# A planner's costs for the products with V are set to other values, and the whole order is searched again

## The chip, the cores and the metric

The kernel runs on one core of a Trainium2 chip. The metric is the device time of one execution in microseconds (us). Besides it there is a profile of one execution, taken by the hardware profiler: its span runs from the first to the last instruction, and the execution's own time is a little longer than the span.

## The reference, cut to what matters

Two independent parts are computed from different inputs and set side by side in the output, in float32:

```python
# A: attention, S = 2048 rows, D = 1024, H = 32 heads of 32
qkv = (x @ wqkv)                      # split into q, k, v by head
p = softmax(einsum("bhqd,bhkd->bhqk", q, k) * 32 ** -0.5)
o = einsum("bhqk,bhkd->bhqd", p, v)
a = o.reshape(B, S, D) @ wo
# B: real part of a two-dimensional Fourier transform by four matrices
u = einsum("bsd,ed->bse", xb, dft_hid_re); w = einsum("bsd,ed->bse", xb, dft_hid_im)
b = einsum("ts,bse->bte", dft_seq_re, u) - einsum("ts,bse->bte", dft_seq_im, w)
out = concatenate([a, b], -1)
```

## The kernel before

All dense products (q, k and v, the Fourier products, the product with wo) are done by a fast scheme with fewer block products (seven for eight, nested), and each product of float32 tiles is three matmuls of a high and a low half (hi*hi, lo*hi, hi*lo) into one PSUM bank. In the profile these matmuls have line L457. They are called fills here; there are 6528, each with 512 moving columns, and they stand in one list `fills` in a fixed order. What a fill reads is made ahead of it: a load by a queue of SyncE (SP), sums by DVE or POOL (L522), the high half by a cast on ACT (L542) or DVE (L544), the low half by a subtraction on POOL or DVE (L547). The tiles are called slot (moving) and hl (stationary).

The attention runs at the same time, head by head, and is three streams of PE work:

- S (L1896): 32 pairs of matmuls a head, scores of 128 queries against 1024 keys into one of two psS tiles. DVE takes the row maximum (L1902), ACT the exponent with a sum (L1905, an ACTIVATE and a read of the accumulator), after which the tile is free for the S pair after next. S only finds maxima and sums. Most pairs read their queries from the tile qs, the first four rows of a head from qx.
- T (L2018): 64 matmuls a head, the transposed scores less the maximum, one at a time into one of two psT banks. ACT takes the exponent (L2022) into a tile pt.
- V (L2037): the products with v. They stand in runs, three to a head, of 5, 5 and 6 key tiles (`ENDS`); a key tile is four matmuls in four column groups of 32 of the array, and the profile shows each of these as two. A run of 5 tiles is thus x40 in the profile and x20 in the program.

Every instruction is an `Op` with a cost in us, an engine and what it waits for. A planner (`Plan`, `run`) goes through time by these costs and decides which instruction comes next on each engine: whenever PE is free it takes a fill, or the head of one of the streams S, T and V, by readiness and some rules. What it writes is a fixed order for each engine. On the chip the engines go through their orders one instruction after another, and semaphores hold an instruction until its inputs are there; the planned times themselves are not used on the chip.

A fill that is not ready by the plan is passed over, and PE goes on with S and T alone. A place where T follows T with no fill between them, next to an S and not just behind a run of V, is called a bare pair here.

The planner's rules have eight numbers that a random search tunes: 90 trials (`TRIALS`), each a dry run of the whole plan, and the one with the shortest planned total is emitted. Two of the eight: `LATE` is the margin that PE leaves after an operand's planned readiness, and `RES` is how many fills are kept for the end. The cost of a run of V enters in two ways:

```python
v = op("PE", SWITCH + (t + 1 - t0) * PV, pv, [*load[: t // 4 + 1], *(x[3] for x in todo)], [vuse, *(x[4] for x in todo)])
ATT = H * (128 * MS + 16 * PV + 3 * SWITCH)
if fill is not None and (not ok or (not first and left <= HB) or nf / (FILL - RES) <= done / ATT):
```

The second of them is the total planned PE time of the attention, by which the fills are spread over it.

Of the kernel before, what the change touches and what calls it, by code (L numbers as in the profile page):

```python
# [253 lines left out]
def kernel(  # L254
# [128 lines left out]
    ORDER = (1, 2, 5, 6, 7, 3, 4)  # L383
    OUTERS = [(0, q) for q in (1, 5, 6, 7, 3, 2, 4)] + [(1, q) for q in ORDER]
    TWO = {(1, q) for q in ORDER} | {(0, 2), (0, 4)}
    MM, MS, PV, SWITCH, TINY = 0.2165, 0.2165, 0.853, 0.40, 0.17
    ES, ET = 1.222, 0.61
    MAX, EVAC, CAST, BIT = 1.22, 0.685, 0.415, 0.275
    SUB = 1.31
# [1843 lines left out]
```

## Time and profile before

| | |
|---|---|
| median of 3 runs | 2829.85 us (2828.16 to 2834.0) |
| the profiled execution, its own time | 2831.55 us |
| its span | 2829.8 us |
| PE busy | 2797.1 us (99%) |
| DVE busy, ACT busy, POOL busy | 2377.2, 2355.6, 1191.7 us |
| bytes moved by DMA | 768.18 MB, mean 271 GB/s |
| mean granted TensorE clock | 0.998 |

A busy share is the time in which at least one instruction of the engine is under way. Matmuls overlap in the profile, one of 512 columns being shown for 380 ns or so while the next one starts some 216 ns after it. How much of PE's time is lost is therefore read from the starts of the matmuls.

### The profile page before, as it was taken

How to read it: one execution, taken by the hardware profiler on the slowest of the kernel's cores; microseconds unless marked ns; L12 is line 12 of the kernel's file. 1: busy time of each engine (PE TensorE's matmuls, PEld its weight loads, DVE VectorE, ACT ScalarE, POOL GpSimd, SP SyncE). 2: the span in 40 equal slices, each digit the busy share in tenths (PEclk: the TensorE clock that was granted, in tenths of full speed). 3: DMA queues.
4: the chain of work that ended last, by engine and by line, in shares of the span. 5: the costliest groups of instructions: out<-in, count | busy, mean ns of one | idle time of the engine just before them, and what ended most of it. 6: DMA issues, size and time to landing. Idle time of an engine off the chain costs nothing.

```text
span 2829.8 us, 47069 instructions
## 1 busy us (share of the span) xinstructions
PE 2797.1 (99%) x14728; PEld 2095.6 (74%) x14728; DVE 2377.2 (84%) x3300; ACT 2355.6 (83%) x4490; POOL 1191.7 (42%) x945
## 2 busy tenths in 40 slices
PE   9999999999999999999999999999999999999999
PEld 8787777776777777677676777767767777777777
DVE  6678888788888888798988899888888998888845
ACT  5348898998899899889999988999988988888851
POOL 2234434133234432356545446676765331343300
PEclk9999999999999999999999999999999999999999
DMA  9989978798899988977999767888867665677548
GB/s 345 344 312 305 316 249 293 252 337 298 300 302 344 333 298 297 296 232 231 335 342 339 251 207 241 293 270 266 277 179 237 220 211 185 203 237 252 178 154 296
DMA packets 485844, 768.18 MB, mean 271 GB/s; under 512 B 120382, under 2 KB 153406, under 8 KB 485470
## 3 DMA queue, kind: packets, MB, share of 16 engines
q1 hardware_dynamic: 485452, 765.04, 81.6%
q8 instruction: 119, 1.95, 0.3%
q14 instruction: 129, 1.06, 0.1%
q10 hardware_dynamic: 144, 0.13, 0.0%
HBM read 511.74 MB, written 253.25 MB: 270 GB/s over the span
## 4 chain that ended last, share of the span: by engine, by line
PE 88%; DMA 5%; ACT 3%; DVE 2%; issue 1%; POOL 1%; SPq 1%; DVEq 0%; POOLq 0%; ACTq 0%
PE pd L457 40%; PE pd L2037 15%; PE psT L2018 15%; PE psS L1896 14%; PE psT L457 4%; ACT psS L1905 2%; ACT pt L2022 1%; DVE negm L1902 1%; DMA ha_d<-slot 1%; DMA ha_d<-c 0%; DMA c<-in_xb 0%; DMA raw<-in_xa 0%; DMA slot<-in_ct 0%; DMA qs<-qk_d 0%; DMA raw<-in_wv 0%
## 5 line engine op out<-in xcount | busy, mean ns | idle before, releaser
L457 PE MATMUL pd<-slot,hl 128*128 128x512 f32 x5088 | 1412.1, 380 | 4.0 <-ACT hl L542 2.0
L2022 ACT ACTIVATE pt<-psT 128x512 f32<-128x512 f32 x2048 | 1215.3, 689 | 228.8 <-PE psT L2018 227.3
L1902 DVE TENSOR_REDUCE negm<-psS 128x1 f32<-128x1024 f32 x1024 | 1241.5, 1219 | 169.2 <-PE psS L1896 153.8
L1905 ACT ACTIVATE psS<-psS,negm 128x1024 f32<-128x1024 f32 x1024 | 1225.1, 1197 | 41.6 <-DVE negm L1902 40.7
L457 PEld LDWEIGHTS pd<-slot,hl 128*128 128x128 f32 x5088 | 963.8, 190 | 133.3 <-ACT hl L542 2.4
L2018 PE MATMUL psT<-qs,ks 128*128 128x512 f32 x2048 | 786.0, 387 | 1.2 <-DMA r_d<-ll 0.7
L2018 PEld LDWEIGHTS psT<-qs,ks 128*128 128x128 f32 x2048 | 383.2, 188 | 168.8 <-issue 46.9
L1896 PE MATMUL psS<-ks,qs 128*128 128x512 f32 x1552 | 457.9, 381 | 9.1 <-ACT psS L1905 8.9
L2037 PE MATMUL pd<-pt,vt 128*32 128x512 f32 x4096 | 459.3, 594 | 2.8 <-DVE e L766 1.8
L547 POOL TENSOR_TENSOR slot<-raw,slot 128x512 fp32r<-128x512 f32 x153 | 194.9, 1279 | 353.8 <-DVE slot L547 98.8
L547 POOL TENSOR_TENSOR slot<-slot,slot 128x512 fp32r<-128x512 f32 x206 | 260.4, 1280 | 196.3 <-DVE slot L544 50.1
L1896 PEld LDWEIGHTS psS<-ks,qs 128*128 128x128 f32 x1552 | 283.7, 189 | 66.4 <-ACT psS L1905 21.3
L2037 PEld LDWEIGHTS pd<-pt,vt 128*32 128x32 f32 x4096 | 123.9, 110 | 281.4 <-issue 261.3
L1905 ACT ACTIVATION_READ_ACCUMULATOR psS<-psS,negm 128x1 f32 x1024 | 324.8, 317 | 0.0
L522 POOL TENSOR_TENSOR raw<-raw,g 128x512 f32<-128x512 f32 x114 | 145.4, 1279 | 231.9 <-DMA g<-tg_d 23.6
L547 POOL TENSOR_TENSOR hl<-raw,hl 128x512 fp32r<-128x512 f32 x113 | 144.4, 1279 | 214.8 <-PE psT L2018 62.0
L457 PE MATMUL pd<-slot,slot 128*128 128x512 f32 x780 | 200.8, 379 | 0.0
L457 PEld LDWEIGHTS pd<-slot,slot 128*128 128x128 f32 x780 | 147.4, 189 | 20.1
L1896 PE MATMUL psS<-ks,qx 128*128 128x512 f32 x496 | 146.5, 386 | 6.1 <-ACT psS L1905 5.3
L1896 PEld LDWEIGHTS psS<-ks,qx 128*128 128x128 f32 x496 | 90.0, 189 | 34.9 <-ACT psS L1905 10.9
L522 DVE TENSOR_TENSOR raw<-raw,g 128x512 f32<-128x512 f32 x146 | 106.9, 740 | 9.1 <-issue 2.2
L2050 DVE TENSOR_TENSOR ot<-ot,pd 128x512 f32<-128x512 f32 x64 | 43.9, 686 | 68.7 <-PE pd L2037 67.9
(139 smaller groups left out, 2135.0 us busy)
## 6 DMA issues: line engine op xcount, KB each, us to landing
hl<-ha_d SPq DMA_DIRECT2D x134, 512.0 KB
slot<-in_ct SPq DMA_DIRECT2D x144, 256.0 KB
qk_d<-e SPq DMA_DIRECT2D x52, 512.0 KB
qs<-qk_d SPq DMA_DIRECT2D x128, 192.0 KB
ks<-qk_d SPq DMA_DIRECT2D x128, 192.0 KB
raw<-g_d SPq DMA_DIRECT2D x96, 256.0 KB
ha_d<-hl SPq DMA_DIRECT2D x42, 512.0 KB
raw<-in_ct SPq DMA_DIRECT2D x80, 256.0 KB
```

Of the source, the lines that this page charges most:

```text
L457: nc.tensor.matmul(box["ps"], a[1]((a[0].hi, a[0].lo)[u]()), turns((b[0].hi, b[0].lo)[v]()), start=k == 0, stop=k == n - 1)
L522: (nc.gpsimd if e == "POOL" else nc.vector).tensor_tensor(out=dest(), in0=dest() if a is None else a.get(), in1=other["q"] if "q" in other ...
L547: (nc.gpsimd if e == "POOL" else nc.vector).tensor_tensor(out=lo(), in0=raw(), in1=f(hi()), op=ALU.subtract)
L1896: nc.tensor.matmul(p[:, i * NB : i * NB + NB], (QX[0] if own else QS[h % 2])[:, qt * P : qt * P + P], turns(KS[h % 2][:, c * 1024 + i * NB ...
L1902: nc.vector.tensor_reduce(out=ST["negm"][:, c, qt : qt + 1], in_=box["p"], axis=AX.X, op=ALU.max, negate=True)
L1905: nc.scalar.activation(box["p"], box["p"], AF.Exp, bias=ST["negm"][:, c, qt : qt + 1], accum_out=ST["sums"][:, c, qt : qt + 1])
L2018: nc.tensor.matmul(box["p"], KS[h % 2][:, t * P : t * P + P], turns(QS[h % 2][:, j * NB : j * NB + NB]), start=True, stop=True)
L2022: nc.scalar.activation(box["t"], box["p"], AF.Exp)
L2037: nc.tensor.matmul(po["p"][j * DH : j * DH + DH, :], VT[h][:, k, :], box["t"], start=(k == t0), stop=(k == t), tile_position=(0, j * DH),)
L2050: nc.vector.tensor_tensor(out=as_two(po["o"]), in0=as_two(po["o"]), in1=order_of(po["p"]), op=ALU.add)
```

## The change

Two costs of the planner get other values: `PV`, a key tile of a run of V, and `SWITCH`, what a run costs beyond its tiles. Nothing else in the source differs.

```diff
-    MM, MS, PV, SWITCH, TINY = 0.2165, 0.2165, 0.853, 0.40, 0.17
+    MM, MS, PV, SWITCH, TINY = 0.2165, 0.2165, 0.858, 0.337, 0.17
```

A run of 5 tiles is planned at 0.337 + 5 x 0.858 = 4.627 us, where it was 0.40 + 5 x 0.853 = 4.665; a run of 6 at 5.485, where it was 5.518. As every planned time behind the first run moves, the dry runs come out differently and the search ends at another trial: before it took `LATE` 0.239 and `SST` 13.89 (a ratio of the streams S and T) with the other six at their defaults (`RES` 700), now it takes `LATE` 0.177 and `RES` 567 with the others at their defaults. The instructions are the same except where an operation may go to one of two engines (ACT has 18 more, DVE 20 fewer, POOL 2 more); their order differs on every engine. On PE there are 21 bare pairs before and 29 now; 351 fills stand behind the last instruction of the attention before, 307 now.

On PE, near fill 2976 of 6528, where the group of fills that reads slot_14254 begins (slot_14293 is the same tile in the new program). Before:

```order
L457 MATMUL pd<-slot_13722,hl 128x512
L1896 MATMUL psS<-ks_2705,qs_2704 128x512 x2
L2018 MATMUL psT<-qs_709,ks_710 128x512
L457 MATMUL pd<-slot_13722,hl 128x512
L2018 MATMUL psT<-qs_709,ks_710 128x512
L457 MATMUL pd<-slot_13722,hl 128x512
L457 MATMUL pd<-slot_14254,hl 128x512 x2
L1896 MATMUL psS<-ks_2705,qs_2704 128x512 x2
L457 MATMUL pd<-slot_14254,hl 128x512
```

Now, at the same fills:

```order
L457 MATMUL pd<-slot_13702,hl 128x512
L2018 MATMUL psT<-qs_709,ks_710 128x512
L1896 MATMUL psS<-ks_2708,qx 128x512 x2
L2018 MATMUL psT<-qs_709,ks_710 128x512 x2
L1896 MATMUL psS<-ks_2708,qs_2707 128x512 x2
L2018 MATMUL psT<-qs_709,ks_710 128x512 x2
L1896 MATMUL psS<-ks_2708,qs_2707 128x512 x2
L2018 MATMUL psT<-qs_709,ks_710 128x512 x2
L1896 MATMUL psS<-ks_2708,qs_2707 128x512 x2
L2018 MATMUL psT<-qs_709,ks_710 128x512
L457 MATMUL pd<-slot_14293,hl 128x512 x2
```

Four S pairs and eight T stand where there were fills between them: three bare pairs.

On PE, at fill 3301, eleven fills ahead of a place at fill 3312 where four bare pairs stand in both orders (slot_15744 before and slot_15785 now are one tile). Before:

```order
L457 MATMUL pd<-slot_15744,hl 128x512
L1896 MATMUL psS<-ks_2705,qs_2704 128x512 x2
L2018 MATMUL psT<-qs_709,ks_710 128x512
L457 MATMUL pd<-slot_15744,hl 128x512
L2018 MATMUL psT<-qs_709,ks_710 128x512
L457 MATMUL pd<-slot_15744,hl 128x512
```

Now:

```order
L457 MATMUL pd<-slot_15785,hl 128x512
L1896 MATMUL psS<-ks_2708,qx 128x512 x2
L2018 MATMUL psT<-qs_709,ks_710 128x512 x2
L1896 MATMUL psS<-ks_2708,qx 128x512 x2
L2018 MATMUL psT<-qs_709,ks_710 128x512 x2
L1896 MATMUL psS<-ks_2708,qs_2707 128x512 x2
L2018 MATMUL psT<-qs_709,ks_710 128x512
L457 MATMUL pd<-slot_15785,hl 128x512 x2
```

The last two of these three fills now stand behind three S pairs and five T, with two bare pairs among them.

On ACT, where the scores of the second head begin; each L1905 is the exponent of one S pair, and the casts L542 make operands of fills. Before:

```order
L1905 ACTIVATE psS,sums<-psS,negm 128x1024 x3
L542 ACTIVATE slot_3026<-raw 128x512
L542 ACTIVATE hl<-raw 128x512
L1905 ACTIVATE psS,sums<-psS,negm 128x1024 x2
L1961 ACTIVATE tt<-tt 128x32
```

Now:

```order
L1905 ACTIVATE psS,sums<-psS,negm 128x1024 x2
L542 ACTIVATE slot_3028<-raw 128x512
L1905 ACTIVATE psS,sums<-psS,negm 128x1024
L542 ACTIVATE e<-e 128x512
L1334 ACTIVATE c<-c 128x512
L542 ACTIVATE hl<-raw 128x512
L1905 ACTIVATE psS,sums<-psS,negm 128x1024
```

The first cast to hl stood ahead of the 32nd exponent and now stands behind it, ahead of the 33rd.

## Rows read from the trace of the kernel before

**Rows 1.** The page: span, and PE (busy us, share, instructions).

```profile
span 2829.8 us, 47069 instructions
PE 2797.1 (99%) x14728; PEld 2095.6 (74%) x14728; DVE 2377.2 (84%) x3300; ACT 2355.6 (83%) x4490; POOL 1191.7 (42%) x945
```

**Rows 2.** Groups by line, PE: the products with V.

```profile
L2037 PE MATMUL pd<-pt,vt 128*32 128x512 f32 x4096 | 459.3, 594 | 2.8 <-DVE e L766 1.8 <-DVE slot L714 0.8 <-DVE e L1012 0.2
```

**Rows 3.** Timeline of PE after the attention: start us, us, what, count.

```profile
2755.55 10.52 PE L457 MATMUL pd<-slot,hl 128*128 128x512 f32 x48
2765.91 10.52 PE L457 MATMUL psT<-slot,hl 128*128 128x512 f32 x48
...
2821.59 1.46 PE L457 MATMUL pd<-slot,slot 128*128 128x512 f32 x6
```

**Rows 4.** Timeline of PE around one run of V of six tiles.

```profile
2368.00 0.81 PE L457 MATMUL pd<-slot,slot 128*128 128x512 f32 x3
2368.74 5.36 PE L2037 MATMUL pd<-pt,vt 128*32 128x512 f32 x48
2374.03 0.70 PE L2018 MATMUL psT<-qs,ks 128*128 128x512 f32 x2
2374.56 1.03 PE L1896 MATMUL psS<-ks,qx 128*128 128x512 f32 x4
```

**Rows 5.** Timeline of PE in the four bare pairs at fill 3312.

```profile
1366.24 0.92 PE L2018 MATMUL psT<-qs,ks 128*128 128x512 f32 x2
1367.77 0.70 PE L1896 MATMUL psS<-ks,qs 128*128 128x512 f32 x2 [0.61 <-ACT psS L1905]
1368.31 0.92 PE L2018 MATMUL psT<-qs,ks 128*128 128x512 f32 x2
1369.84 0.70 PE L1896 MATMUL psS<-ks,qs 128*128 128x512 f32 x2 [0.61 <-ACT psS L1905]
```

**Rows 6.** Timeline of ACT in the same stretch, one cycle.

```profile
1366.41 1.19 ACT L1905 ACTIVATE psS<-psS,negm 128x1024 f32<-128x1024 f32 x1
1367.41 0.31 ACT L1905 ACTIVATION_READ_ACCUMULATOR psS<-psS,negm 128x1 f32 x1
1367.50 1.19 ACT L2022 ACTIVATE pt<-psT 128x512 f32<-128x512 f32 x2
1368.46 1.21 ACT L1905 ACTIVATE psS<-psS,negm 128x1024 f32<-128x1024 f32 x1
```

**Rows 7.** Windows, PE alone: stretch, length, busy (matmuls), clock, DMA share, GB/s.

```profile
1129.30:1133.70 4.40, 3.17 (x10) 1.00 0.89 279
1364.20:1371.20 7.00, 5.33 (x17) 1.00 1.07 343
...
1888.50:1891.10 2.60, 1.97 (x6) 1.00 0.90 332
...
116.00:136.00 20.00, 15.45 (x59) 0.91 1.01 353
238.00:248.00 10.00, 7.43 (x27) 0.83 0.90 319
```

**Rows 8.** PE's waits over the whole span: total us, times, longest.

```profile
PE psS L1896 <- ACT psS L1905: 14.2, 23, 2.6
```

**Rows 9.** Timeline of PE, two waits within 116 to 136 us.

```profile
119.02 0.48 PE L457 MATMUL pd<-slot,hl 128*128 128x512 f32 x1 [1.99 <-ACT hl L542]
...
128.46 2.64 PE L457 MATMUL psT<-slot,hl 128*128 128x512 f32 x11 [1.27 <-DVE hl L547]
```

**Rows 10.** Timeline of all engines where the second head's scores begin.

```profile
237.93 2.84 SPq L506 DMA_DIRECT2D raw<-in_wqk  x2
...
240.91 0.63 ACT L542 ACTIVATE hl<-raw 128x512 fp32r<-128x512 f32 x1 [1.85 <-DMA raw<-in_wqk]
241.45 1.07 ACT L1905 ACTIVATE psS<-psS,negm 128x1024 f32<-128x1024 f32 x1
...
242.69 0.48 PE L1896 MATMUL psS<-ks,qx 128*128 128x512 f32 x1 [2.57 <-ACT psS L1905]
```

## Prediction

> **What bounds the kernel now.** I read the page first. TensorE (PE) is busy 99% of the span, 2797.1 of 2829.8 us, and ACT and DVE 83 and 84% [rows 1]. So PE sets the time, but its busy share says too little about what can still move: the profile shows a matmul for some 380 ns while the next one starts after 216. The timeline after the attention gives the pitch: 48 fills take 2765.91 - 2755.55 = 10.36 us, 0.2158 us each [rows 3]. Next I looked at one run of V. The three fills ahead of it should be done issuing at 2368.00 + 3 x 0.2158 = 2368.65; V starts at 2368.74, 0.09 later; it lasts until 2374.03, 5.29 us for six tiles; the two T behind it take 0.53 us where two pitches are 0.43, so leaving costs another 0.10 [rows 4]. Together 5.48 us.
>
> With these, all the work of PE can be added up. Of 14728 matmuls 4096 are V [rows 1, 2]. The other 10632 at 0.2158 us are 2294.4 us. V is 512 tiles at 0.858 and 96 runs at 0.337, 471.7 us. The sum is 2766.1 us; the span holds 63.7 us more. Of these 6.8 lie behind PE's last matmul, which ends at 2821.59 + 1.46 = 2823.05 [rows 3], and the rest is lost by PE. The change can only work on this rest, because it adds and removes no matmul.
>
> The Trainium skill (Perfetto Trace Analysis, Identifying the Most-Contended Engine) says that matmul busy time is a poor measure of what PE has left, since the instructions are pipelined. The rows here agree: by busy time 32.7 us are open, by the starts 63.7.
>
> Where is it lost? Three kinds of place stand out.
>
> (a) Bare pairs. Where no fill stands between S and T, PE runs into ACT. One cycle of ACT is one exponent, its accumulator read and two exponents of T: from 1366.41 to 1368.46, 2.05 us [rows 6]. PE starts an S pair every 2.07 us there and has only four matmuls, 0.86 us, to do in it [rows 5]. A full bare cycle thus loses 1.2 us. By windows: at fill 3312 four bare pairs take 7.00 us with 17 matmuls, 3.67 us of work, so 3.33 are lost, 0.83 a pair (the first one is cheap, since ACT is not behind yet). At 1129 us two pairs lose 4.40 - 10 x 0.2158 = 2.24, 1.12 each; at 1888 us one loses 2.60 - 6 x 0.2158 = 1.30 [rows 7].
>
> (b) The early stretch, where DMA is full (share 1.01): 116 to 136 us holds 59 matmuls, 12.7 us of work in 20, so 7.3 are lost; 238 to 248 us holds 27, so 4.2 are lost [rows 7]. In the first, PE waits for operands (1.99 and 1.27 us) [rows 9]. In the second, ACT's cast to hl waits for its weights, the exponent of an S pair stands behind it, and PE waits 2.57 us for that exponent [rows 10]. In both the granted clock falls, to means of 0.91 and 0.83 [rows 7]: that is 0.09 x 20 = 1.8 and 0.17 x 10 = 1.7 us, already within the losses.
>
> (c) Single waits elsewhere; the list has 23 waits of S for ACT, 14.2 us, the longest 2.6, bare pairs included [rows 8].
>
> **The change, part by part.** The table itself. The new values are right: a run of six tiles is planned at 5.485 us, measured 5.48, before 5.518 [rows 4]. The plan's clock no longer gains 0.033 to 0.038 us a run on the chip's, over 96 runs 3.5 us. On the chip this is worth nothing in itself, 0 us: a run lasts as long as it lasts, and semaphores set both clocks together again at each wait. What hides the old error is that a fixed order with waits needs no clock; 0.04 us is a fifth of one matmul. So the 3.5 us that leave the planned total do not leave the chip's.
>
> The new order: bare pairs. What reaches the chip is another order, found by a search that goes by the planned total. On PE it has 29 bare pairs in place of 21. The new ones are three at fill 2976, two at fill 3301 (ahead of the four at 3312, which stay), and more in ones and twos; some late ones are gone. Price of a pair: nothing, if the chip would have waited at that place anyway; 1.2 us at most, a full cycle [rows 5]; the three windows gave 0.83, 1.12 and 1.30 [rows 7]. I take 0.9, the lower part, because several of the new pairs stand alone. 8 x 0.9 = +7.2 us, bounds 0 and +9.6. ACT also gets 18 casts more, at 0.63 us [rows 10] 11 us over the whole span; it has 17% of the span free [rows 1], and what hides them is that they stand between fills; in a bare stretch they would lengthen the cycle, which is one reason not to go lower than 0.9.
>
> The new order: the second head's start. The first cast to hl now stands behind the 32nd exponent, so the S pair that waited for it is released, and the next one waits, some 2 us of PE work later. Of the wait of 2.57 us [rows 10] about 0.6 should be left. Gain between 0 (if other loads come later on SP) and 4.2 (all that is lost there, its clock too [rows 7]). I take -2.
>
> The early stretch, 116 to 136 us: SP's order has the same 72 rows from row 93 on in both programs, which are the loads of this stretch, and DMA is full there. I put 0.
>
> `LATE` at 0.177 in place of 0.239 lets PE take an operand 0.06 us nearer to its planned readiness, `RES` at 567 keeps fewer fills for the end. Fewer fills at the end (307 for 351) cost nothing: at the end a fill takes its pitch, as it does elsewhere [rows 3], so a fill costs 0.2158 us wherever it stands between others. The smaller margin can turn into small waits; nothing in the trace prices it apart. From below it is 0; from above, 23 waits of S for ACT [rows 8] each longer by 0.06 are 1.4. I take 0.
>
> Other single waits (c) are dealt anew, with no reason for a sign: 0, and some 5 us either way for the range.
>
> Sum: 7.2 - 2 = +5.2 us. Against the profiled execution (2831.55 us, its span and 1.75 around it) this is 2836.7; its own time lies 1.7 above the median of the runs shown, and I forecast the median: 2829.85 + 5.2 = 2835.0 us. I call faster or slower what differs by over 0.2%, 5.7 us, about what a measurement of this kernel can tell from no change: below 2824.2 or above 2835.5. The forecast lies just inside.
>
> **The rivals.** Slower: the bare stretches cost their full price. Place: fills 2976 and 3301 to 3312, where the new order has bare stretches of four and of seven cycles with little between the latter. Price: 8 x 1.2 = 9.6, nothing gained at the second head: 2839.5; if PE's clock also falls there, 1.7 us a time by the fall at 238 us [rows 7], twice: 2843. It decides from some 0.96 us a pair on if the gain of 2 holds, and from 0.71 without it. For it: cycles that follow the first cost 1.2. Against the clock's part: in 7 us with four bare pairs the clock stayed at 1.00 [rows 7].
>
> The Trainium skill (TensorE: Matmul & The Clock Gate, HAM oscillation) warns that an array which idles between bursts of matmuls is gated back to half its clock, 1.2 for 2.4 GHz, again and again. The trace shows such falls only near the waits at 119 and 240 us, where PE stood still for 2 us and more; by this rule the longer bare stretches would bring the 2843 above.
>
> No effect: a bare pair takes the place of a wait that the chip had anyhow, because the fill behind it is late on the chip too, and the makers of later fills get ahead meanwhile. Then the 8 pairs cost about 0 and the second head's gain is small: 2828 to 2831. For it: of the 63.7 us only part lies in bare pairs, so other waits can shrink.
>
> Faster: casts and exponents no longer stand in PE's way in the early stretch. Place: 116 to 136 and 238 to 248 us; price 7.3 + 4.2 = 11.5 us with the clock [rows 7], 2818 if bare pairs cost nothing. It decides when the weights' casts come earlier by the 2.0 to 2.6 us of these waits [rows 9, 10] and a bare pair costs under 0.7. Against it: the loads of the first stretch have the same order, and DMA has no room there.
>
> **How the numbers follow.** Forecast, 2832 to 2838: 0.40. Slower, 2838 to 2845: 0.22. No effect, 2826 to 2832: 0.23. Faster, 2816 to 2826: 0.15. Faster by over 0.2%: most of the last, 0.13. Slower: the second and somewhat under half of the first, 0.39. Within: 0.48. The range 2823 to 2842 leaves out about 0.10 below and 0.08 above; the likeliest case alone has 2832 to 2838.
>
> **What would show it.** In the changed kernel's profile: a run of V as before, 5.29 us for six tiles. S pairs 2.07 us apart, with waits of 0.6 for ACT, for four cycles near 1206 us and for some three more just ahead of the four near 1364 us; there PE's lost time should be 3 and 2 us where before it was none. Near 240 us the wait for the exponent under 1 us. At 116 to 136 us again 7 us lost. It would be wrong if the waits outside the bare pairs changed by more than 6 us in sum, if the new bare stretches showed PE work at its full pitch, or if PE's waits at V or at fills for DVE grew, where the trace of before has few.

## The result and the profile after

The changed kernel takes 2836.66 us, the median of 14 runs (2831.94 to 2840.95); the kernel before took 2829.72 in 14 runs of its own (2827.24 to 2834.01). The medians differ by 6.9 us. The ratio taken over the runs, which is not the quotient of the two medians (that is 1.0025), is 1.0019 with a 95% interval of 1.0012 to 1.0026, some 3 to 7 us: slower, and at the edge of the 0.2% by which the prediction told slower from no change. The forecast was 2835.0, that is +5.2. The profiled execution took 2838.27 us.

**A correction first.** The section on the change names the search's settings the wrong way round. The kernel before runs with `LATE` 0.177 and `RES` 567, and the changed kernel with `LATE` 0.239, `SST` 13.89 and `RES` 700. Experiments 6, 7 and 9 below show it: with these settings put in by hand, PE's order is the one in the trace of the kernel before (9) and of the changed kernel (6 and 7), matmul for matmul. The orders shown, the 21 and 29 bare pairs and the 351 and 307 fills at the end are those of before and of the change, as stated. The prediction's two terms on `LATE` and `RES` thus argue from the wrong sign (the margin became larger, not smaller). Both were put at 0, so the sum does not change; the 1.4 us that bounded the margin's part from above would have bounded it from below.

The page of the changed kernel, against [rows 1, 2]:

```profile
span 2836.5 us, 47037 instructions
PE 2800.3 (99%) x14728; PEld 2102.3 (74%) x14728; DVE 2370.5 (84%) x3280; ACT 2366.6 (83%) x4508; POOL 1196.2 (42%) x947
L2037 PE MATMUL pd<-pt,vt 128*32 128x512 f32 x4096 | 460.0, 595 | 1.2 <-DVE e L766 0.7
```

By busy time nothing can be told: PE is 99% busy in both. PE's last matmul starts at 2830.4 us where it started at 2822.7, 7.7 us later, so all of the difference is PE time lost between matmuls. The waits of PE, against [rows 8]:

```profile
PE psS L1896 <- ACT psS L1905: 15.7, 34, 1.1
PE psT L2018 <- DMA qs<-m_d: 5.7, 5, 2.6
PE pd L457 <- ACT hl L542: 2.5, 1, 2.5
```

S now waits for ACT 34 times and not 23, while the longest of these waits has gone from 2.6 to 1.1 us. What has grown most is the second line, from 0.4 us in one wait to 5.7 us in five: T waits for the queries in qs, into which the maxima have been written back by DMA.

The windows of PE that the prediction had named, and one behind the third of them:

```profile
1206.10:1212.90 6.80, 4.92 (x15) 1.00 1.06 318
1364.30:1369.10 4.80, 3.60 (x14) 1.00 1.01 276
1372.10:1379.00 6.90, 5.05 (x15) 0.94 1.05 354
1378.00:1386.00 8.00, 7.83 (x47) 0.79 0.67 197
116.00:136.00 20.00, 15.10 (x60) 0.91 1.02 361
238.00:248.00 10.00, 9.46 (x43) 1.00 0.96 355
```

With 0.2158 us for each matmul, the first three stretches lose 6.80 - 15 x 0.2158 = 3.6, 1.8 and 3.7 us. The early stretch loses 7.1 us as before (7.3), and 238 to 248 us loses 0.7 where it lost 4.2 [rows 7]. Once PE has started, the granted clock (1.00 is 2.4 GHz) falls at two places of each profiled execution: in the early stretch in both (mean 0.91), and then near 240 us before and near 1378 us after.

The timeline of PE at fill 2976, where the first new bare pairs stand:

```profile
1206.12 0.70 PE L1896 MATMUL psS<-ks,qx 128*128 128x512 f32 x2 [0.22 <-ACT psS L1905]
1206.66 0.92 PE L2018 MATMUL psT<-qs,ks 128*128 128x512 f32 x2
1208.20 0.70 PE L1896 MATMUL psS<-ks,qs 128*128 128x512 f32 x2 [0.61 <-ACT psS L1905]
...
1212.34 0.70 PE L1896 MATMUL psS<-ks,qs 128*128 128x512 f32 x2 [0.61 <-ACT psS L1905]
1212.87 0.44 PE L2018 MATMUL psT<-qs,ks 128*128 128x512 f32 x1
1213.15 0.59 PE L457 MATMUL pd<-slot,hl 128*128 128x512 f32 x2
```

and of DVE there:

```profile
1211.24 1.22 DVE L1902 TENSOR_REDUCE negm<-psS 128x1 f32<-128x1024 f32 x1
1212.38 0.42 DVE L544 CAST slot<-slot 128x512 fp32r<-128x512 f32 x1
1212.83 0.69 DVE L547 TENSOR_TENSOR slot<-slot,slot 128x512 fp32r<-128x512 f32 x1
```

S pairs are 2.07 us apart with waits of 0.61 us, as in [rows 5]. The cast of the fill's operand ends at 1212.80 and the fill starts at 1213.15: the operand is late on the chip too, not only in the plan. It stands behind a maximum in DVE's order, and the sum ahead of that maximum, from which it is made, waited 0.31 us for POOL.

The timeline of PE where the stretch at fill 3312 ends:

```profile
1376.10 0.70 PE L1896 MATMUL psS<-ks,qs 128*128 128x512 f32 x2 [0.61 <-ACT psS L1905]
1376.64 0.92 PE L2018 MATMUL psT<-qs,ks 128*128 128x512 f32 x2
1378.17 1.21 PE L1896 MATMUL psS<-ks,qs 128*128 128x512 f32 x2 [0.61 <-ACT psS L1905]
1379.17 1.06 PE L2018 MATMUL psT<-qs,ks 128*128 128x512 f32 x2
1380.16 5.20 PE L2037 MATMUL pd<-pt,vt 128*32 128x512 f32 x40
1385.29 0.70 PE L2018 MATMUL psT<-qs,ks 128*128 128x512 f32 x2
```

Behind these bare pairs matmuls start some 0.5 us apart and not 0.216, with no wait between them, and the granted clock from 1378 to 1386 is 0.79 on the mean: for part of it PE ran at 1.2 GHz. The run of five tiles takes 5.13 us. In the kernel before, the run of five tiles behind the four bare pairs took 1375.65 - 1371.22 = 4.43 us, at a clock of 1.00:

```profile
1371.22 4.50 PE L2037 MATMUL pd<-pt,vt 128*32 128x512 f32 x40
1375.65 0.48 PE L2018 MATMUL psT<-qs,ks 128*128 128x512 f32 x1
```

ACT where the second head begins, against [rows 10]:

```profile
238.79 1.07 ACT L1905 ACTIVATE psS<-psS,negm 128x1024 f32<-128x1024 f32 x1
...
240.93 0.61 ACT L542 ACTIVATE hl<-raw 128x512 fp32r<-128x512 f32 x1
241.44 1.07 ACT L1905 ACTIVATE psS<-psS,negm 128x1024 f32<-128x1024 f32 x1
```

The cast to hl now stands behind the exponent, and the S pair waits 0.53 us at 240.03 where one waited 2.57.

**The lost time of PE, by traces.** I took every interval between the starts of two matmuls in each trace, subtracted a pitch (0.2155 us; 0.31 into and 0.522 out of a run of V), and separated what lies in bare stretches from the rest. The absolute sums stand some 11 us above the prediction's, because the 0.10 us behind each of the 96 runs counts as lost here and the pitch is a little lower; only differences are used. Each row comes from one execution; runs of one order differ by up to 9 us (2831.94 to 2840.95 in the changed kernel), so a difference of a few us between two rows can be scatter.

| profiled execution of | bare pairs | lost there, us | each | lost elsewhere | sum | median us of the runs |
|---|---|---|---|---|---|---|
| before | 21 | 19.5 | 0.93 | 49.1 | 68.5 | 2829.72 |
| after | 29 | 27.3 | 0.94 | 48.8 | 76.1 | 2836.66 |
| new_table_old_settings | 26 | 25.1 | 0.96 | 65.1 | 90.1 | 2849.73 |
| old_table_new_settings | 30 | 28.0 | 0.93 | 45.3 | 73.3 | 2836.03 |
| old_table_defaults | 17 | 21.2 | 1.25 | 59.9 | 81.1 | 2845.02 |
| new_table_seed2 | 20 | 20.6 | 1.03 | 52.9 | 73.5 | 2836.43 |
| bare_pairs_added | 98 | 95.2 | 0.97 | 38.4 | 133.6 | 2895.38 |
| after_order_half_exp | 29 | 19.4 | 0.67 | 37.3 | 56.7 | 2822.90 |
| after_order_half_max | 29 | 24.7 | 0.85 | 38.8 | 63.5 | 2828.20 |
| half_max_replanned | 7 | 7.6 | 1.09 | 41.7 | 49.3 | 2807.68 |
| one_cast_moved | 21 | 20.4 | 0.97 | 48.3 | 68.7 | 2828.26 |
| old_table_searched_longer | 18 | 17.6 | 0.98 | 49.2 | 66.7 | 2827.11 |
| new_table_searched_longer | 17 | 20.1 | 1.18 | 48.6 | 68.7 | 2833.80 |

From before to after: bare pairs +7.8 us; what is lost elsewhere before 260 us 17.0 to 12.7, -4.3; what is lost elsewhere behind 260 us +4.0.

### The profile page after: what moved, and what is told of

Read it like the earlier page. It is cut to its first block, busy times and chain, and to the rows that moved or that the text cites. A ratio compares the mean times of both kernels' runs of the same rounds, so it can differ in the third digit from the quotient of the medians.

```text
span 2836.5 us, 47037 instructions
## 1 busy us (share of the span) xinstructions
PE 2800.3 (99%) x14728; PEld 2102.3 (74%) x14728; DVE 2370.5 (84%) x3280; ACT 2366.6 (83%) x4508; POOL 1196.2 (42%) x947
## 4 chain that ended last, share of the span: by engine, by line
PE 84%; ACT 6%; DMA 5%; DVE 2%; issue 1%; SPq 1%; POOL 0%; DVEq 0%; POOLq 0%; ACTq 0%
PE pd L457 38%; PE pd L2037 14%; PE psT L2018 14%; PE psS L1896 13%; PE psT L457 4%; ACT psS L1905 4%; ACT pt L2022 2%; DMA hl<-ha_d 1%; DVE negm L1902 1%; DMA qs<-m_d 1%; DMA m_d<-lt 0%; DMA g<-in_ct 0%; DMA g<-g_d 0%; DMA g<-tg_d 0%; DMA g<-t_d 0%
## 5 line engine op out<-in xcount | busy, mean ns | idle before, releaser
L1905 ACT ACTIVATE psS<-psS,negm 128x1024 f32<-128x1024 f32 x1024 | 1218.8, 1191 | 63.3 <-DVE negm L1902 61.2
L1896 PE MATMUL psS<-ks,qs 128*128 128x512 f32 x1552 | 458.6, 382 | 12.4 <-ACT psS L1905 11.5
L1905 ACT ACTIVATION_READ_ACCUMULATOR psS<-psS,negm 128x1 f32 x1024 | 317.7, 310 | 0.0
L522 POOL TENSOR_TENSOR raw<-raw,g 128x512 f32<-128x512 f32 x118 | 151.9, 1289 | 211.0 <-issue 22.2
L1375 POOL TENSOR_TENSOR slot<-slot 128x512 f32<-128x512 f32 x34 | 43.9, 1294 | 124.8 <-DMA v_d<-e 36.6
```

The lines of the kernel that those rows point to most:

```text
L522: (nc.gpsimd if e == "POOL" else nc.vector).tensor_tensor(out=dest(), in0=dest() if a is None else a.get(), in1=other["q"] if "q" in other ...
L1375: made = op("POOL", SUB, lambda e, part=part, kind=ALU.add if terms[1][0] > 0 else ALU.subtract: (nc.gpsimd if e == "POOL" else nc.vector) ...
L1896: nc.tensor.matmul(p[:, i * NB : i * NB + NB], (QX[0] if own else QS[h % 2])[:, qt * P : qt * P + P], turns(KS[h % 2][:, c * 1024 + i * NB ...
L1905: nc.scalar.activation(box["p"], box["p"], AF.Exp, bias=ST["negm"][:, c, qt : qt + 1], accum_out=ST["sums"][:, c, qt : qt + 1])
```

## The experiments

Ratios are to the kernel before, run in the same comparison, with a 95% interval. Its median lay between 2828.65 and 2829.72 us in the four comparisons, so a distance to the changed kernel, which ran in the first of them alone, is good to about 1 us. In the cuts of the code settings are rounded, and `...` stands for what is left out. In the first four, the search is replaced by given settings, so that table and order come apart.

**1. The new table with the settings of before** (in the changed kernel).

```diff
-    best, shortest = {}, run(True)
...
+    best = dict(LATE=0.1766, RES=566.6)
```

> The new costs with the settings that the search took before (LATE 0.177, RES 567), no search. The order has 26 bare pairs on PE (before 21, after 29). Theory (the time follows the bare pairs, about 1.0 us each; before loses 20.1 us in 21 of them): 2829.7 + 5 x 1.0 = 2835 us, within 5. Rival 1 (the settings decide, since the smaller margin packs PE closer): as before, 2830 us. Rival 2 (the table decides, a right table gives an order that suits the chip worse or better whatever the settings): as after, 2837 us. Rival 3 (the waits outside the bare pairs, dealt anew by every order, decide): no relation to 26, anywhere from 2825 to 2850.

Measured: 2849.73 us, 1.0073 (1.0060 to 1.0085). The price by bare pairs gave 2835 and missed by 15 us. Its waits of PE:

```profile
PE psS L1896 <- ACT psS L1905: 18.8, 34, 1.9
PE psT L2018 <- DMA qs<-m_d: 5.2, 4, 2.3
```

With five pairs more than before, the bare stretches lose 5.6 us more, as priced; what is lost elsewhere grew by 16. Part of that is the clock. It falls in four stretches and not two: its mean is 0.83 from 238 to 248 us, 0.66 from 638 to 648 and 0.79 from 1396 to 1404 and from 1508 to 1516. A run of V of six tiles that starts at 641.21 us takes 8.23 us for 5.29.

**2. The old table with the settings of after** (in the kernel before).

```diff
+    best = dict(LATE=0.2391, SST=13.886)
```

> The old costs with the settings that the search took for the new ones (LATE 0.239, SST 13.89), no search. 30 bare pairs. Theory (1.0 us a bare pair): 2829.7 + 9 = 2839 us, within 5. Rival 1 (settings decide): as after, 2837 us. Rival 2 (the table decides): as before, 2830 us. Rival 3 (other waits decide): anywhere from 2825 to 2850.

Measured: 2836.03 us, 1.0025 (1.0016 to 1.0034). With the old values in the table the time is that of the changed kernel. The two values alone are therefore not what costs the 7 us; an order that these settings give costs it with either table.

**3. The old table with all settings at their defaults** (in the kernel before).

```diff
+    best = {}
```

> The old costs with the default settings (LATE 0.25, RES 700), no search. 17 bare pairs, the fewest of the four. Theory (1.0 us a bare pair): 2829.7 - 4 = 2826 us, within 5, faster than before. Rival 2 (the table decides): 2830 us. Rival 3 (other waits decide): an order that no search has picked is expected slower, 2835 to 2850, with losses outside its bare pairs above the 48 us of before.

Measured: 2845.02 us, 1.0051 (1.0039 to 1.0063), with the fewest pairs of the four. By bare pairs it should have been the fastest. Its waits of PE show kinds that neither kernel has at this size:

```profile
PE psS L1896 <- ACT psS L1905: 18.3, 32, 2.1
PE psS L1896 <- DMA ks<-qk_d: 4.7, 3, 2.9
PE pd L457 <- POOL hl L547: 2.2, 2, 1.2
```

**4. The new table, another draw of the search** (in the changed kernel).

```diff
+    best = {'PATIENCE': 0.711, 'STOCK': 2.286}
```

> The new costs with the settings that the same search finds from another seed of its random numbers (PATIENCE 0.711, STOCK 2.286, the rest at their defaults). 20 bare pairs. Theory (1.0 us a bare pair): 2829.7 - 1 = 2829 us, within 5: the new table is then no slower than the old one, and what was measured is the draw of the search. Rival 2 (the table decides): as after, 2837 us. Rival 3 (other waits decide): anywhere from 2825 to 2850.

Measured: 2836.43 us, 1.0030 (1.0019 to 1.0041). With 20 pairs, one less than before, it is no faster than the changed kernel with 29.

With these four the theory that the number of bare pairs sets the time from one order to the next has fallen. A pair has its price, but what is lost elsewhere moves by up to 16 us from order to order.

**5. Bare pairs added to the order of before.** The plan's order is kept as a list and emitted from there; at 33 places the middle fills of a group are moved together ahead of its last one, so that the S and T between them stand bare (33 groups with no run of V inside).

```diff
+        middle = g[1:-1]
...
+        moved[g[-1]] = middle
...
+    todo_list = [x for r in todo_list if r[0] not in gone for x in ([by[o] for o in moved.get(r[0], ())] + [r])]
...
-    run(False, **best)
...
+    for o, e, dep, att_on[0], t_on[0] in todo_list:
+        o.emit(e) if o.other else o.emit()
```

> The order of before, emitted from a recorded list, with one edit on PE alone: in 33 groups of 12 or 24 fills the fills between the first and the last are moved behind the S and T that stood among them. No instruction is added, the orders of ACT, DVE, POOL and SP stay. 98 bare pairs in place of 21. Theory (a bare pair costs its ACT cycle, 0.83 to 1.2 us, and what is lost there doesn't come back): 77 x 1.05 = 81 us more, 2910 us, between 2890 and 2920. Rival (a bare pair takes the place of a wait that comes later anyway, since ACT, DVE and the makers of operands get ahead in it): under 20 us more, below 2850.

Measured: 2895.38 us, 1.0245 (1.0231 to 1.0259), against 2828.65 in the same comparison: +66.7 us for 77 pairs, 0.87 each (by the ratio 69 us, 0.90 each). In the table, the bare stretches lose 75.7 us more (0.98 each) and the rest 10.7 less. One of the places in the timeline of PE:

```profile
604.10 0.70 PE L1896 MATMUL psS<-ks,qs 128*128 128x512 f32 x2
604.63 0.92 PE L2018 MATMUL psT<-qs,ks 128*128 128x512 f32 x2
606.16 0.70 PE L1896 MATMUL psS<-ks,qs 128*128 128x512 f32 x2 [0.61 <-ACT psS L1905]
606.70 0.92 PE L2018 MATMUL psT<-qs,ks 128*128 128x512 f32 x2
607.46 3.19 PE L457 MATMUL pd<-slot,hl 128*128 128x512 f32 x14
```

The pairs are paid even where the fills were not late, and about a seventh comes back at other waits. So the price of 0.9 is shown with the rest of the order held. The theory's 1.05 was too high: 0.98 is lost at the places, and part of it comes back.

**6. The order of after, emitted from a list as in 5, the exponent of S over half its columns** (the sums leave out half of the keys):

```diff
-    nc.scalar.activation(box["p"], box["p"], AF.Exp, ...)
+    nc.scalar.activation(box["p"][:, :NB], box["p"][:, :NB], AF.Exp, ...)
```

> The order of after, unchanged on every engine; the exponent of an S pair on ACT is taken over 512 of its 1024 columns (the sums leave out half of the keys). Theory 1 (the length of a bare stretch is set by ACT's cycle): the cycle falls from 2.07 to some 1.6 us, a bare pair from some 1.07 to 0.6, 14 us less in 29 pairs and some single waits for ACT gone: 2820 us, between 2815 and 2826. Theory 2 (the stretch ends when the operand of the fill behind it is made, and that is late through DVE, whose queue is full there): PE then waits at the fill in place of at S, 0 to 5 us less, 2834 us.

Measured: 2822.9 us, 0.9987 (0.9979 to 0.9995), 13.8 us below the changed kernel. The timeline of PE at fill 2976:

```profile
1196.49 0.70 PE L1896 MATMUL psS<-ks,qs 128*128 128x512 f32 x2 [0.52 <-ACT psS L1905]
1197.03 0.92 PE L2018 MATMUL psT<-qs,ks 128*128 128x512 f32 x2
1198.46 0.70 PE L1896 MATMUL psS<-ks,qs 128*128 128x512 f32 x2 [0.51 <-ACT psS L1905]
1198.99 0.43 PE L2018 MATMUL psT<-qs,ks 128*128 128x512 f32 x1
1200.06 0.70 PE L457 MATMUL pd<-slot,hl 128*128 128x512 f32 x2 [0.63 <-DVE slot L544]
```

and of ACT:

```profile
1195.66 0.66 ACT L1905 ACTIVATE psS<-psS,negm 128x512 f32<-128x512 f32 x1 [0.23 <-DVE negm L1902]
...
1197.63 0.66 ACT L1905 ACTIVATE psS<-psS,negm 128x512 f32<-128x512 f32 x1 [0.22 <-DVE negm L1902]
```

and of DVE:

```profile
1194.35 1.22 DVE L1902 TENSOR_REDUCE negm<-psS 128x1 f32<-128x1024 f32 x1
1195.48 0.92 DVE L547 TENSOR_TENSOR hl<-raw,hl 128x512 fp32r<-128x512 f32 x1
1196.32 1.21 DVE L1902 TENSOR_REDUCE negm<-psS 128x1 f32<-128x1024 f32 x1
```

The exponent takes 0.66 us and not 1.2, yet the pairs are still 1.97 us apart: ACT now waits for DVE's maximum, whose own cycle with one subtraction is 1.97 us, and at the end the fill waits 0.63 us for DVE. At this place almost nothing is gained, since DVE stands right behind ACT. The gain of the whole comes from both sides of the table (bare 7.9, elsewhere 11.5), so the run does not split the cause cleanly.

**7. The same order, DVE's maximum over half the columns** (the maxima leave out half of the keys):

```diff
-    nc.vector.tensor_reduce(out=..., in_=box["p"], ...)
+    nc.vector.tensor_reduce(out=..., in_=box["p"][:, :NB], ...)
```

> The order of after, unchanged on every engine; DVE's maximum of an S pair is taken over 512 of its 1024 columns (the maxima leave out half of the keys). DVE loses some 530 us of its 2370 us of work. Theory 1 (with the order fixed, ACT's cycle sets the bare stretches): nothing there, 3 us or so of single waits for DVE, 2833 us, between 2829 and 2837. Theory 2 (late operands from DVE hold PE in the bare stretches also where the trace names ACT): 10 us less or more, below 2827.

Measured: 2828.2 us, 1.0001 (0.9993 to 1.0010), 8.5 us below the changed kernel. The bare stretches lose only 2.6 us less, since with the order held ACT's cycle sets them; the other 10 come from elsewhere. The time lies between the two theories.

**8. The same half maximum, and the plan told of it**; the search is made anew in the changed kernel.

```diff
-    MAX, EVAC, CAST, BIT = 1.22, 0.685, 0.415, 0.275
+    MAX, EVAC, CAST, BIT = 0.69, 0.685, 0.415, 0.275
```

> The kernel after with DVE's maximum taken over 512 of 1024 columns (the maxima leave out half of the keys), its planned cost set to 0.69 in place of 1.22, and the order searched anew in 90 trials. 7 bare pairs are left of 29, so the planner left fills out because DVE was to make their operands too late. Theory (the bare pairs come from DVE, and their loss goes with them): 24 us less in bare pairs, the rest dealt anew: 2812 us, between 2804 and 2820. Rival (bare pairs are a symptom; the waits elsewhere take over): 2830 us or more.

Measured: 2807.68 us, 0.9934 (0.9922 to 0.9946), 29 us below the changed kernel. The page and the waits of PE:

```profile
PE 2783.3 (99%) x14728; PEld 2115.0 (75%) x14728; DVE 2135.4 (76%) x3643; ACT 2307.7 (82%) x4399; POOL 879.3 (31%) x693
PE psS L1896 <- ACT psS L1905: 4.6, 8, 0.9
```

Seven bare pairs are left of 29. Of the 29 us, experiment 7 gave 8.5 with the order held; the rest comes with the new order. So it is DVE's load as planned that makes the planner leave fills out and put pairs bare; ACT, with DVE close behind it (6), sets what each then costs. POOL's work shrank too, from 1196.2 to 879.3 us, since operations went over to DVE; what POOL's slower operations contribute to late operands is not shown apart.

**9. The order of before, one exponent moved ahead of the cast to hl** (`x` is the 32nd exponent of S in ACT's order, `cast` the operation ahead of it).

```diff
+    todo_list.insert(cast, todo_list.pop(x))
```

> The order of before, emitted from a recorded list, with one edit: on ACT the first cast to hl at 240 us stands behind the 32nd exponent in place of ahead of it, as it does in after. 21 bare pairs as before. Theory (that cast held the exponent and PE, and let the clock fall): 3 us less, 2826 us, and 238 to 248 us holds some 40 matmuls in place of 27. Rival (the next exponent waits in its place, or the time comes back at a later wait): 0, 2829 us.

Measured: 2828.26 us, 0.9991 (0.9981 to 1.0000), against 2829.35. The windows of PE:

```profile
238.00:248.00 10.00, 9.12 (x41) 1.00 0.98 346
116.00:136.00 20.00, 15.23 (x53) 0.83 0.98 335
```

At the place itself 41 matmuls stand where there were 27, and the clock is 1.00 where it was 0.83: 14 x 0.2158 = 3.0 us gained. The whole gained 1.1 us by the medians and 2.5 us by the ratio, with an interval from 0 to 5.4 us: it fits the 3.0, and is hardly told from nothing. In this execution the stretch from 116 us lost more than before (53 matmuls for 59), which the moved cast cannot reach.

**10 and 11. A longer search, about 3000 trials with the old table and 3600 with the new one.** The first line stands in the kernel before, the second in the changed one.

```diff
+    best = {'LATE': 0.179, 'SFIRST': 0.606, 'SST': 13.25, 'LEAD': 2.00, 'RES': 564, 'STOCK': 1.80, 'PATIENCE': 0.489}
+    best = {'LATE': 0.268, 'PATIENCE': 0.678, 'STOCK': 1.64, 'SST': 12.26, 'LEAD': 2.28, 'RES': 660}
```

> The old costs with settings from a search of some 3000 trials in place of 90 (LATE 0.179, SFIRST 0.606, SST 13.25, LEAD 2.00, RES 564, STOCK 1.80, PATIENCE 0.489). 18 bare pairs. Theory (time is base, plus 0.95 us a bare pair, plus a rest that each order deals anew and that lay between 45 and 65 us in six orders so far; a search that goes by the planned total also lowers the rest): 2827 us, between 2822 and 2834. Rival (the search's total says nothing about the rest on the chip): 2835 to 2845.

> The new costs with settings from a search of some 3600 trials (LATE 0.268, PATIENCE 0.678, STOCK 1.64, SST 12.26, LEAD 2.28, RES 660). 17 bare pairs. Theory: as the kernel searched longer with the old costs, 2828 us, between 2822 and 2835; the table then makes no difference once the search is long. Rival 1 (the right table gives an order that suits the chip better): 2820 or less. Rival 2 (the search's total says nothing about the rest): 2835 to 2845.

Measured: 2827.11 us, 0.9994 (0.9985 to 1.0003), and 2833.80 us, 1.0016 (1.0006 to 1.0025). The longer search leaves 18 and 17 bare pairs, and with the better fitting table the kernel is still no faster than before. The expectation that the table makes no difference once the search is long was not borne out: the two are 6.7 us apart, with about the same number of bare pairs. No version that does the whole work beat the kernel before by more than its interval.

## Why the prediction came out as it did, by its own steps

- *The table itself, 0.* Experiment 2 bears it out as far as one order can: old values and new settings give 2836.03 us, new values and new settings 2836.66. Experiment 1 and the kernel before have the same settings and different values, and differ by 21 us; but their orders differ, so that is the order's doing too. That the planned times fit the chip better brought no visible gain in any of the four orders made with the new values and the full work.
- *Eight bare pairs at 0.9, +7.2.* The traces give +7.8, that is 0.98 for each pair more, and experiment 5 0.87 each net in another order. About 1.0 of the 7.8 is the clock's fall at 1378 us. The cycle of 2.07 us stands at fill 2976 as forecast; the losses there and ahead of fill 3312 are 3.6 and 1.8 us, for 3 and 2 forecast. The rival of the full price of 1.2 is thus refuted for its price. Of its clock part, one fall of two came in the profiled execution: from 1378.17 to the run at 1380.16 four matmuls and the entry take 1.99 us for 0.95, and the run 5.13 for 4.43, together 1.7 us lost, the size taken from the fall at 238 us. It took what the second head's start had given back: two falls before, two after.
- *The second head's start, -2.* Mis-sized: that stretch lost 3.5 us less, and all of PE before 260 us 4.3 less. The wait left, 0.53 us, is the 0.6 forecast; what the term left out is the clock, which stays at 1.00 when the long wait is gone. The bound of 4.2 held it.
- *116 to 136 us, 0.* Right: 7.1 us lost for 7.3. This was the place that the faster rival needed.
- *`LATE` and `RES`, 0.* Argued from the wrong sign, as said above, and not shown apart by any run.
- *Single waits, 0 with 5 either way.* They came to +4.0. Of this one wait stands out, in the timeline of PE:

```profile
1117.10 0.70 PE L1896 MATMUL psS<-ks,qx 128*128 128x512 f32 x2
1120.42 0.70 PE L2018 MATMUL psT<-qs,ks 128*128 128x512 f32 x2 [2.62 <-DMA qs<-m_d]
```

  T follows a run of V and two S pairs, and its queries are not written back yet. Another 0.7 us is the slower run of V behind 1378 us (5.13 us for 4.43).

The sum, 7.8 - 4.3 + 4.0 = 7.5 us, is what PE's last matmul moved by (7.7), as it must be, since both come from the same two traces. That it came close to +5.2 is partly luck: the two errors of 2.3 and 4.0 us have opposite signs, and experiment 1 shows that the last term could have been some 16, where the prediction's range allowed 5.

Why the better values did not help is settled only in part. Shown: a bare pair costs 0.87 us net where 77 were added to one order, they come from DVE's planned load, and the rest moves by up to 16 us from order to order, more than the 3.5 us of planned time that the edit corrects. Argued and not shown: that the old settings were a lucky draw, kept because they happened to be short on the chip as well; six other orders from the planner ran at 2827 to 2850 us. A rival stands beside it. Of the orders that a search picked, the two with the old values ran at 2829.7 and 2827.1 us, and the three with the new ones at 2836.7, 2836.4 and 2833.8. So it is not excluded that the new values themselves lead the search to slower orders, for instance because the 0.03 to 0.04 us by which each run of V was planned too long worked as a margin. Five draws are too few to tell. What makes the waits elsewhere in experiment 1 so many stays open, but for the clock's part.

## What to carry to other kernels

When a change reaches the chip only through a search over orders, price the order that came out, place by place, and give the rest of the order a range as wide as other draws of the same search show; a few of these, run ahead, tell more than the edit does. A cost table that fits better need not bring anything by itself where semaphores set the order's pace; here 3.5 us of planned time were smaller than the spread from order to order. To learn what a pattern costs, hold the order and add the pattern many times: 77 pairs settled the price that 8 left within the scatter.

## What the hardware showed that I had not expected

The clock fell behind four bare pairs at 1378 us, with no wait longer than 0.61 us just ahead, whereas behind the same four pairs in the kernel before the clock stayed at 1.00 to the end of the window [rows 7] and through the run of V behind it. The Trainium skill (TensorE: Matmul & The Clock Gate, HAM oscillation) says that an array that waits for DMA between its bursts of matmuls falls back to half its clock at each of them. The waits in a bare stretch are for ACT and far shorter, so the prediction stretched that rule when it tied the 2843 us to it. The trace of the changed kernel shows a fall behind bare pairs once, at 1378 us, and not at 1206 us, where three bare pairs ran at 1.00; and with 98 pairs the mean granted clock of experiment 5 is 0.998, the same as before with 21.

ACT and DVE are nearly equal limits in a bare stretch: with the exponent at 0.66 us in place of 1.2 the cycle shrank from 2.07 to 1.97 us at fill 2976, because DVE's cycle of a maximum and one subtraction, 1.97 us, came next.
